# Attention and gated MLP on one core: K's first transposes moved ahead of x, weight loads held until x has landed, far loads held behind a copy of K

## The chip, the cores and the metric

One core of one Trainium2 chip. The metric is the device time of one execution in microseconds (us). Runs of one kernel mostly agree within 0.1%. In the lines of the profile PE is TensorE, PEld its weight loads, DVE VectorE, ACT ScalarE, POOL GpSimd and SP SyncE; L393 is line 393 of that run's kernel. A transfer lands when its data has arrived.

## The reference, cut to what matters

x is 2048 x 640. It is layer-normalised and goes into two branches: attention with 32 heads of size 192 against a cache of 2048 keys and values, and a gated MLP whose gate and up products share x.

```
xn = layernorm(x)
q = (xn @ wq) in 32 heads of 192;  p = softmax(q k^T / sqrt(192));  s = (p v) @ wo
g = silu((silu(xn @ w1) * (xn @ w3)) @ w2)
return x + s * g
```

## The kernel before

TensorE runs almost without a gap for 1.9 ms. Only the start concerns us: x, K and V of head 0 and the first weights must come in, x must be normalised and transposed, K transposed, before the first scores. TensorE does its part of it in program order.

```
def turn_over(k):                     # filler: keeps TensorE busy so that its clock rises
    for i in range(k):
        nc.tensor.matmul(warm, lhsT=ident_bf[:], rhs=ident_bf[:], start=True, stop=True)

def ln_turn(g, i2, copy):             # transposes two of the four tiles of an x group
    pst = ps_st.tile([P, 2, DC, P], BF16, tag="st2", name="pst")
    # ... 10 transposes into pst
    copy(out=xnT[:, :, q0:q0 + 2 * P]..., in_=pst[:])

def swap_halves(g):                   # xnS: the same x with its two partition halves exchanged
    qs = slice(g * 512, (g + 1) * 512)
    nc.sync.dma_start(out=xnS[0:64, :, qs], in_=xnT[64:P, :, qs])
    nc.sync.dma_start(out=xnS[64:P, :, qs], in_=xnT[0:64, :, qs])

def project_first():
    for hh in range(2):               # hh 0 reads the first half of x only
        hs = slice(hh * 256, (hh + 1) * 256)
        ps = ps_st.tile([P, 1024], F32, tag="st2", name="ps0")
        # ... 10 matmuls on xnT[:, c, hs], then casts by VectorE and ScalarE

def head_start():
    load_x(0, 0, 2); load_x(0, 2, 4); load_k0(0, nc.sync)
    load_w0()                         # three loads issued by GpSimd
    turn_over(44)
    # ... statistics of x
    load_k0(1, nc.scalar)             # K's second half
    load_x(1, queue=nc.scalar)        # the far loads: x of group 1 and half of V,
    load_v(0, (0,), nc.scalar)        # needed later
    # ... statistics, load_w(1), normalise
    ln_turn(0, 0, nc.scalar.copy)
    turn_k0(pk0, 0, range(4))         # 16 transposes: K's first half
    ln_turn(0, 1, nc.vector.tensor_copy)
    turn_k0(pk1, 1, (0, 1))           # 8 transposes: K's second half
    swap_halves(0)
    copy_k0(nc.scalar.copy, pk0, 0, 0)
    # ... two more copies of K, load_v(0, (1,)), load_x(2)
    project_first()
    # ... scores
```

The tiles pst, ps0 and the scores take turns in one pool of PSUM buffers (tag st2; PSUM is the memory that the matmuls here write to).

## Time and profile before

| | kernel before |
|---|---|
| time, median of its first 3 runs | 1938.25 us |
| span of the profiled run | 1936.4 us |
| TensorE busy | 1926.6 us |
| first projection, first scores, first product with V | 10.15, 13.10, 14.74 us |
| projection for head 1, projection of x group 1 | 18.84, 24.84 us |

The last row is times from the start of the span at which landmarks on TensorE begin. All waits of TensorE in the first 60 us (engine and line, what it waited for: us, times, longest):

```profile
PE pk L572 <- POOL ident_bf masks.py:199: 2.8, 1, 2.8
PE pst L354 <- DVE xn L346: 0.9, 1, 0.9
PE st L483 <- DVE qA L393: 0.2, 1, 0.2
```

There is not one wait for a transfer. That looks like slack, and it is not: the second view, a timeline of TensorE at head 1's projection (start, length, what), shows the first reader of xnS.

```profile
18.84 0.38 PE L424 MATMUL ps<-xnT,W 64*128 64x512 bf16 x1
19.05 0.39 PE L424 MATMUL ps<-xnS,W 64*128 64x512 bf16 x2
```

Matmuls on xnT and xnS are written as pairs on the two halves of the array. Here the xnS one starts 0.21 us after its partner: the second transfer of xnS, issued at 11.57, took 7.4 us to land, until about 19.0. Busy times by stretch (stretch, length, then the busy time of TensorE, its weight loads, VectorE, ScalarE and GpSimd with their instruction counts, granted clock, share of the DMA engines' time, GB/s):

```profile
5.00:6.00 1.00, 1.00 (x17) 1.00 (x16) 0.93 (x5) 0.97 (x3) 0.00 (x0) 1.00 0.99 298
6.00:7.00 1.00, 0.66 (x12) 0.49 (x9) 0.93 (x4) 0.45 (x2) 0.72 (x1) 1.00 0.74 155
```

### The profile page before, as it was taken

The page shows a single profiled execution, that of the slowest core. Times are in us where ns is not written, and L with a number is a line of the kernel's source. Part 1 is how long each engine was busy: PE and PEld are TensorE (multiplying, and loading weights), DVE is VectorE, ACT ScalarE, POOL GpSimd, SP SyncE. Part 2 cuts the span into 40 slices and gives each one's busy share as a digit, 9 for nine tenths or more (in the row PEclk, how much of TensorE's full clock was granted, in tenths as well). Part 3 has the DMA queues.
Part 4 walks back from the last instruction along what each step waited for, and adds up shares of the span by engine and source line. Part 5 has one row for each costly group of instructions (what it writes and reads, how often), then busy time and mean ns, then how long its engine had stood idle before and what let it go on. Part 6 is the DMA issues. An engine that isn't in the chain of part 4 may idle for free.

```text
span 1936.4 us, 59669 instructions
## 1 busy us (share of the span) xinstructions
PE 1926.6 (99%) x27273; PEld 1315.6 (68%) x27281; DVE 654.6 (34%) x997; ACT 1180.0 (61%) x1279; POOL 282.5 (15%) x501
## 2 busy tenths in 40 slices
PE   9999999999999999999999999999999999999998
PEld 6666666666666666666666666666666666577776
DVE  7333333333333333333333333333333334521111
ACT  6677676767676767776777777677767677210000
POOL 3111111111111111111111111111111110000000
PEclk9999999999999999999999999999999999999999
DMA  8643433323333434363434343434334220937783
GB/s 181 129 101 67 98 68 86 84 62 88 59 90 61 100 63 97 68 162 69 101 66 100 69 101 69 101 64 101 69 69 96 58 68 2 260 69 137 151 152 62
DMA packets 394643, 178.98 MB, mean 92 GB/s; under 512 B 341616, under 2 KB 382832, under 8 KB 394384
## 3 DMA queue, kind: packets, MB, share of 16 engines
q1 hardware_dynamic: 371136, 125.32, 31.6%
q0 software_dynamic: 19472, 45.71, 10.0%
q8 instruction: 215, 3.52, 0.8%
q10 hardware_dynamic: 3776, 4.06, 0.7%
q14 instruction: 44, 0.36, 0.1%
HBM read 52.82 MB, written 27.79 MB: 42 GB/s over the span
## 4 chain that ended last, share of the span: by engine, by line
PE 99%; DVE 1%; DMA 0%; ACT 0%; issue 0%; DVEq 0%; ACTq 0%
PE obank L519 35%; PE st L487 34%; PE ps L424 14%; PE ps_s L111 11%; PE ps_f L731 3%; PE ps_gu L705 1%; PE st L488 1%; PE ps L410 0%; DVE stats L316 0%; DMA x_all<-in_A_x_dram 0%; PE ps L391 0%; PE pst L354 0%; PE pk L271 0%; DVE xn L346 0%; ACT pT L493 0%
## 5 line engine op out<-in xcount | busy, mean ns | idle before, releaser
L493 ACT ACTIVATE pT<-st 128x1024 bf16<-128x1024 f32 (+1 forms) x1025 | 1046.1, 1021 | 250.2 <-PE st L488 234.0
L519 PEld LDWEIGHTS <-pT 64*128 64x128 bf16 x16384 | 711.3, 94 | 242.3 <-ACT pT L493 0.6
L519 PE MATMUL obank<-vt,pT 64*128 64x193 bf16 x16384 | 849.7, 243 | 0.0
L487 PE MATMUL st<-qC,KW 64*128 64x512 bf16 x2046 | 605.6, 376 | 0.1
L528 DVE COPY osum<-obank 128x772 f32<-128x772 f32 x128 | 123.1, 962 | 787.1 <-PE obank L519 787.1
L488 PE MATMUL st<-qB,KW 64*128 64x512 bf16 x1024 | 385.0, 376 | 0.0
L487 PE MATMUL st<-qA,KW 64*128 64x512 bf16 x1022 | 384.3, 376 | 0.1
L488 PE MATMUL st<-qC,KW 64*128 64x512 bf16 x1022 | 384.3, 376 | 0.0
L488 PE MATMUL st<-qA,KW 64*128 64x512 bf16 x1022 | 384.3, 376 | 0.0
L487 PEld LDWEIGHTS <-KW 64*128 64x128 bf16 x3068 | 278.5, 94 | 153.7 <-issue 2.1
L424 PE MATMUL ps<-xnT,W 64*128 64x512 bf16 x1280 | 297.2, 376 | 0.0
L424 PE MATMUL ps<-xnS,W 64*128 64x512 bf16 x1280 | 296.0, 376 | 0.0
L488 PEld LDWEIGHTS <-KW 64*128 64x128 bf16 x3068 | 278.5, 94 | 0.5
L377 POOL DMA_DIRECT2D qC<-qA x124 | 65.4, 528 | 1283.0 <-DVE rl_all L535 1268.2
L430 ACT CAST qB<-ps 128x512 bf16<-128x512 f32 x131 | 76.7, 585 | 228.2 <-PE ps L424 222.6
L111 PE MATMUL ps_s<-wo_sb,oT 128*128 128x384 bf16 (+3 forms) x1535 | 208.8, 299 | 0.1
L424 PEld LDWEIGHTS <-W 64*128 64x128 bf16 x2560 | 122.9, 94 | 121.4 <-issue 0.2
L111 PEld LDWEIGHTS <-oT 128*128 128x128 bf16 x1536 | 148.4, 98 | 60.4
L529 DVE TENSOR_TENSOR osum<-osum,obank 128x772 f32<-128x772 f32 x128 | 122.7, 959 | 13.4
L536 DVE TENSOR_TENSOR ostage<-osum,rl_all 128x768 bf16<-128x768 f32 x128 | 122.7, 958 | 6.3 <-DMA o_scr<-ostage 1.9
L465 DVE SCALAR_TENSOR_TENSOR hT<-pt,qB 64x512 bf16<-64x512 bf16 x64 | 43.8, 684 | 197.4 <-ACT pt L464 197.4
L429 DVE CAST qA<-ps 128x512 bf16<-128x512 f32 x131 | 90.6, 692 | 25.3 <-PE ps L410 7.2
(84 smaller groups left out, 621.9 us busy)
## 6 DMA issues: line engine op xcount, KB each, us to landing
o_scr<-ostage SPq DMA_DIRECT2D x16, 1536.0 KB, 10.6
vt<-in_A_v_cache_dram SPq DMA_DIRECT2D x63, 384.0 KB, 5.9
qC<-qA POOLq DMA_DIRECT2D x248, 64.0 KB, 1.9
qC<-qB POOLq DMA_DIRECT2D x124, 64.0 KB, 2.3
wo_sb<-in_A_wo_dram POOLq DMA_DIRECT2D x1, 7680.0 KB, 36.1
W<-in_A_wq_dram POOLq DMA_DIRECT2D x32, 160.0 KB, 3.6
W<-in_B_w_dram POOLq DMA_DIRECT2D x32, 80.0 KB, 3.3
W<-in_A_wq_dram POOLq DMA_DIRECT2D x32, 80.0 KB, 3.0
```

The source lines that it names most:

```text
L111: nc.tensor.matmul(ps[:, 0:w], lhsT=oT[:, k, :], rhs=wo_sb[:, k, c0:c1], start=(k == 0), stop=(k == OC - 1))
L377: nc.gpsimd.dma_start(out=qC[0:64, half, :], in_=qAB[half][64:P, :])
L424: nc.tensor.matmul(ps[:, r * 512:(r + 1) * 512], lhsT=W[rows, j, :], rhs=xs[rows, j // 2, qs], start=(j == 0), stop=(j == 2 * DC - 1))
L429: a = nc.vector.tensor_copy(out=qAB[0][:], in_=ps[:, 0:512])
L430: b = nc.scalar.copy(out=qAB[1][:], in_=ps[:, 512:1024])
L487: nc.tensor.matmul(st2[:, 0:512], lhsT=ka, rhs=qa, start=r == 0 and nr == 3, stop=r == nr - 1)
L488: nc.tensor.matmul(st2[:, 512:1024], lhsT=kb, rhs=qb2, start=r == 0 and nr == 3, stop=r == nr - 1)
L493: nc.scalar.activation(out=pT2[:, c * w:(c + 1) * w], in_=st2[:, c * w:(c + 1) * w], func=ACT.Exp, scale=att_scale)
L519: nc.tensor.matmul(obanks[r][:, j * 256:j * 256 + DH + 1], lhsT=pT2[r * 64:(r + 1) * 64, t * 512 + j * P:t * 512 + (j + 1) * P], rhs=vt[r ...
L528: nc.vector.tensor_copy(out=osum[:], in_=ov[0])
L529: nc.vector.tensor_tensor(out=osum[:], in0=osum[:], in1=ov[1], op=ALU.add)
L536: nc.vector.tensor_tensor(out=ostage[:, qb * 4:qb * 4 + 4, hg * DH:(hg + 1) * DH], in0=osum[:, :, 0:DH], in1=rl.unsqueeze(2).to_broadcast( ...
```

## The change

The intent: K's first half needs nothing from x, so it is turned while TensorE would only run filler. To make it land early, weights are held back until x has landed (a two-column copy on GpSimd that reads x stands before them), and the far loads stand behind ScalarE's first copy of K. The filler reads a constant tile that is ready earlier, and becomes longer.

```diff
+    fill = const.tile([P, P], BF16, name="fill")
+    nc.vector.memset(fill[:], 1.0)
...
+    gate = const.tile([P, 2], BF16, name="gate")
...
-            nc.tensor.matmul(warm, lhsT=ident_bf[:], rhs=ident_bf[:], start=True, stop=True)
+            nc.tensor.matmul(warm, lhsT=fill[:], rhs=fill[:], start=True, stop=True)
...
         load_k0(0, nc.sync)
+        nc.gpsimd.tensor_copy(out=gate[:], in_=x_sb[:, 0, 0:2])
         load_w0()
-        turn_over(44)
+        turn_over(60)
+        pk0 = ps_o.tile([P, 4, 512], BF16, tag="ob0", name="pk0")
+        turn_k0(pk0, 0, range(4))
...
         load_k0(1, nc.scalar)
+        copy_k0(nc.scalar.copy, pk0, 0, 0)
         load_x(1, queue=nc.scalar)
         load_v(0, (0,), nc.scalar)
...
-        pk0 = ps_o.tile([P, 4, 512], BF16, tag="ob0", name="pk0")
         ln_turn(0, 0, nc.scalar.copy)
-        turn_k0(pk0, 0, range(4))
+        turn_k0(pk1, 1, (0, 1))
         ln_turn(0, 1, nc.vector.tensor_copy)
-        turn_k0(pk1, 1, (0, 1))
         swap_halves(0)
-        copy_k0(nc.scalar.copy, pk0, 0, 0)
```

## The prediction

> **What bounds the kernel now.** I read the page first, then the chain of waits that ended last, cut to the start, then the timeline of the first 15 us with the transfers of the same stretch. The page's busy shares and its chain, shares by engine:
>
> ```profile
> PE 1926.6 (99%) x27273; PEld 1315.6 (68%) x27281; DVE 654.6 (34%) x997; ACT 1180.0 (61%) x1279; POOL 282.5 (15%) x501
> ...
> PE 99%; DVE 1%; DMA 0%; ACT 0%; issue 0%; DVEq 0%; ACTq 0%
> ```
>
> TensorE is busy 1926.6 of 1936.4 us, so all its idle time together is 9.8 us, half a per cent. The change touches no instruction of the steady loop; it can only win in the start, so I read the chain there (start us, length us, what):
>
> ```profile
> 0.75 2.81 DMA x_all<-in_A_x_dram
> 3.58 0.90 DVE stats L316 x2
> ...
> 7.13 0.06 DVE ve L590
> 7.19 0.36 DVE xn L346
> 7.55 0.05 issue
> 7.60 0.81 PE pst L354 x10
> 8.41 0.89 PE pk L271 x16
> 9.30 0.56 PE pst L354 x10
> 9.86 0.45 PE pk L271 x8
> 10.31 2.20 PE ps L391 x20
> 12.51 0.02 issue
> 12.53 0.42 DVE qA L393
> ```
>
> The start has three links. The first load of x lands at 0.75 + 2.81 = 3.56. VectorE then works without a hole on layer-norm statistics (3.58 to 7.19) and on the normalised tiles xn. From 7.60 TensorE works in program order: the first half of x turned, 16 transposes of K's first half (pk, 0.89), the second half of x, 8 of K's second half, and the first projection (L391), after whose casts the first scores start at 13.10. So the 16 transposes of K, which need nothing from x, stand in the path after x. Where the second half of x ended its wait shows in the timeline (start, busy, what):
>
> ```profile
> 8.13 0.90 DVE L346 TENSOR_SCALAR xn<-x_all,mv,rstd 128x640 bf16<-128x640 bf16 x2 [0.23 <-POOL rstd L327]
> 8.45 1.23 ACT L356 COPY xnT<-pst 128x1280 bf16<-128x1280 bf16 x1 [2.00 <-PE pst L354]
> ```
>
> xn is complete at 9.03, and ScalarE's copy of the first half of x, which the first projection reads, at 9.68. Both are limits that remain if K's transposes leave. Last, the transfers between 0 and 4.8 us, then 4.8 and 7.0 us (queue: packets, MB, share):
>
> ```profile
> q1 hardware_dynamic: 368, 0.90, 57.5%
> W<-in_A_wq_dram POOLq DMA_DIRECT2D x1, 160.0 KB, 6.1
> W<-in_A_wq_dram POOLq DMA_DIRECT2D x1, 80.0 KB, 4.6
> ...
> q0 software_dynamic: 146, 0.31, 52.8%
> q1 hardware_dynamic: 64, 0.15, 22.1%
> ```
>
> Until 4.8 us SyncE's queue (q1: x and K's first half) moves alone. The weights, though issued by GpSimd from 1.30 on, appear only after that, on q0, and then take over half of the engines' time while the last 0.15 MB of K's first half trickle in: that load, issued at 1.68, needs 6.0 us and lands at 7.7.
>
> **What the Trainium skill says.** "DMA: Bandwidth & Descriptors", section "Issuing engines are not separate DMA queues": transfers issued from SyncE, ScalarE and GpSimd run on the same 16 DMA engines and interleave. The trace agrees for K's first half (above). It does not show the weights hurting x: they moved nothing until x had landed. Same page, section "Anatomy of one DMA": "any semaphore wait happens on the issuing sequencer before dispatch". So the new one-column copy on GpSimd, which waits for x, holds back the three weight loads behind it, and ScalarE's copy of K, waiting for TensorE, holds back the loads of x and V behind it; this trace has no such pair. "TensorE: Matmul & The Clock Gate", Part 1: the array runs at half clock until it has been busy for about 3.4 us. The trace agrees: the filler starts at 2.77, its matmuls take 314 ns at first and 219 at the end, with last start at 6.4, and all later transposes take 219.
>
> **The change part by part.**
>
> (1) *Filler on a constant tile, 60 instead of 44.* It waited for the identity matrix, which GpSimd finishes at 2.72 behind a weight issue (1.30 to 2.32). A VectorE fill of 128x128 right after 0.82 should take some 0.15 us (the 128x16 one takes 0.07), so TensorE starts near 1.1. Cold pairs come every 83 ns (12 per us in the windows of the trace), so 60 last 5.0 us if cold throughout: end 5.5 to 6.1, instead of 6.66. The array is warm when real work begins, as before. Worth nothing by itself: no wait on this filler is on the path.
>
> (2) *Weights behind x.* Their issues move from 1.30 to 3.65 (x at 3.56 plus a tiny copy), 1.02 + 0.89 + 0.87 = 2.78 us, until 6.43. x lands no earlier, since nothing of theirs ran beside it. K's first half, whose packets had the engines to themselves until about 5, should land near 5.8 instead of 7.7. Two debts. GpSimd's first rstd waits until 6.43 instead of running at 6.00; 6.43 + 0.72 = 7.15 is still before VectorE is free at 7.19, and the second rstd needs 7.19 anyway: cost 0 to 0.1. And the weights land later: in the trace 6.1, 5.2 and 4.6 us after issue under load, 3.6, 3.3 and 3.0 as medians of the run; from issues at 3.65, 4.67 and 5.56 that is 8.6 to 10.2 for the last.
>
> (3) *K's first half before x.* With K at 5.8 and the filler over at 6.0, the 16 transposes take 0.93 and end near 7.0, inside TensorE's present hole (6.66 to 7.60). They leave the path: -0.89. But the program now puts the 8 transposes of K's second half before the second half of x. That second half of K is issued by ScalarE at 5.53 as before and landed at 9.1 (3.6 us) beside part of the x load; now it shares the engines with the 0.33 MB of weights but no longer with x and V. Its 0.39 MB plus the weights at the some 340 GB/s of that stretch is 2.1 us from its first packets at about 6.6: my estimate is a landing at 8.6 to 9.0. So: first half of x 7.60 to 8.41, wait for K to about 8.8, 8 transposes 0.45 to 0.55 to 9.3, x's second half (xn complete at 9.03) 0.56 to 9.9, first projection at 9.9 to 10.0. Before: 10.31. Net -0.35. The floor is ScalarE's xnT copy at 9.68, so no more than -0.6 whatever K does.
>
> (4) *Far loads behind ScalarE's first K copy.* The copy runs near 7.0 to 8.0, before the x copy at 8.45, which it does not delay if the issues (0.45 + 0.70) run beside it, as they ran beside an activation before. The loads of x (group 1) and V leave near 7.1 instead of 5.96, about 1.2 us later. V would land near 13.3 to 13.9; its first reader is at 14.7. The x group is read at 14.29 and landed at 10.8. Both have slack: cost 0. ScalarE's second K copy ends earlier, so the first cast no longer queues behind it (11.44 before), which is not on the path.
>
> Sum: -0.35 in the first projection, and the rest of the start (casts 12.53, scores 13.10, exponentials 14.08) shifts with it, since from there on the chain is made of engine work only. A few hundredths come from hiding K's last 8 transposes no better than before. I put the whole at -0.4 of 1938.25.
>
> **The rivals.**
>
> *The weights become the last wait.* First projection waits for weights at 10.2, or for the second part a little later: gain 0 to 0.1, time 1938.2. For it: the landings of 4.6 to 6.1 us in this very stretch. Against: those loads shared the engines with x and K's first half, and the run's medians are 3.0 to 3.6.
>
> *K's second half is the last wait.* If it lands at 9.6 because the weights now move beside it, the whole second half of x waits behind it in order: projection at 10.7, time 1938.6. For it: the new order on TensorE. Against: twice its bytes were on its queue before, and it still landed at 9.1.
>
> *x lands earlier* because GpSimd no longer works beside it. Then everything moves: 0.3 more, 1937.5. Against: no weight packet before 4.8.
>
> *The gain is swallowed later*, at the waits around 28 to 34 us where ScalarE and VectorE are in the chain. Against: these are chains of engine work, which begin earlier too.
>
> **Range and chances.** Expected gain 0.45 with rival three's chance weighed in: 1937.8. Uncertainty of the mechanism about 0.4, of a median of three some 0.4 (the runs spread from 1937.86 to 1939.1): range 1936.9 to 1938.7. Two per cent is 39 us, and the whole start, before the first scores, lasts 13. No rival comes near it; only a changed clock over the whole run could. Chances: faster 0.005, within 2% 0.99, slower 0.005.
>
> **What would show it.** In the changed kernel: filler starts near 1.1 (step 1); weight issues begin near 3.6 and rstd near 6.4 (2); K's first transposes end near 7.0, before the first transposes of x at about 7.6; the first projection begins at 9.7 to 10.1 (3); first scores near 12.7. It is wrong if the weight loads on TensorE's projection, or K's second half ahead of x's, take a wait of over 0.5 us, or if x lands at a time other than 3.5 to 3.6.

## The result, and the profile after

The changed kernel takes 1941.0 us (median of 6, 1939.79 to 1943.84) against 1938.24 for the kernel before (6 runs, 1937.86 to 1939.1). The ratio is 1.0015, interval 1.0002 to 1.0028: within 2%, but about 2.8 us slower where 0.45 faster was predicted.

The waits of TensorE in the first 60 us of the changed kernel:

```profile
PE pk L575 <- DVE fill L297: 1.1, 1, 1.1
PE ps L393 <- DVE xnT L358: 1.0, 1, 1.0
PE obank L521 <- DMA vt<-in_A_v_cache_dram: 0.8, 1, 0.8
PE pk L271 <- DMA kn<-in_A_k_cache_dram: 0.8, 1, 0.8
PE ps L412 <- DMA xnT<-xn: 0.2, 1, 0.2
```

Three of the five lines are transfers, where there were none. The start in order of time (timeline of all engines, cut):

```profile
1.06 6.27 PE L575 MATMUL pk<-fill 128*128 128x128 bf16 x60 [1.06 <-DVE fill L297]
...
7.17 1.06 PE L271 MATMUL pk<-ident_bf,kn 128*128 128x128 bf16 x16
...
9.65 0.62 PE L271 MATMUL pk<-ident_bf,kn 128*128 128x128 bf16 x8 [0.78 <-DMA kn<-in_A_k_cache_dram]
...
10.87 0.82 DVE L358 COPY xnT<-pst 128x1280 bf16<-128x1280 bf16 x1 [1.48 <-PE pst L356]
...
11.84 2.35 PE L393 MATMUL ps<-xnT,W 128*128 128x256 bf16 x20 [1.01 <-DVE xnT L358]
...
17.32 0.84 PE L521 MATMUL obank<-vt,pT 64*128 64x193 bf16 x16 [0.83 <-DMA vt<-in_A_v_cache_dram]
```

The filler runs to 7.3 us, K's first half is turned from 7.17 on, its second half lands at 9.61 and takes 0.78 us of wait, VectorE copies the second half of x from 10.87 to 11.69, and only then does the first projection start, at 11.84 instead of 10.15. At 17.32 the first product with V has waited 0.83 for V. The same two stretches as before show what happened to the transfers:

```profile
5.00:6.00 1.00, 1.00 (x12) 1.00 (x11) 0.93 (x4) 0.97 (x3) 1.00 (x3) 1.00 0.34 70
6.00:7.00 1.00, 1.00 (x13) 1.00 (x11) 0.97 (x4) 0.40 (x2) 0.98 (x2) 1.00 0.56 175
```

From 5 to 7 us the DMA engines are used 34% and 56% of the time, where they had been used 99% and 74%. Work that stood in that stretch is done later, on top of what comes there anyway. Bytes moved by 8, 12 and 20 us, summed from the trace's transfers: 1.73, 2.99 and 4.74 MB before, 1.47, 2.62 and 4.08 after. The first half of V (issuing queue, KB, us from issue to landing), before and then after:

```profile
vt<-in_A_v_cache_dram ACTq DMA_DIRECT2D x1, 384.0 KB, 6.3
```

```profile
vt<-in_A_v_cache_dram ACTq DMA_DIRECT2D x1, 384.0 KB, 8.6
```

It is issued at 8.64 instead of 6.44 and lands at about 17.3 instead of 12.7. The second transfer of xnS lands at 12.53 + 9.0 = 21.5 instead of 19.0; its reader begins at 21.62, 0.36 after its partner on the array.

From the projection of x group 1 on (27.53 us, 2.69 later than before) the two kernels run in parallel: the spans differ by 2.6. This holds for all variants below. Span minus the start of that projection is 1911.4 to 1911.6 us in 19 of 20 profiles (in e14 0.9 more, not followed up), so that landmark accounts for the whole difference between the profiled runs.

### The profile page after: what moved, and what is told of

Read it like the earlier page. It is cut to its first block, busy times and chain, and to the rows that moved or that the text cites. A ratio compares the mean times of both kernels' runs of the same rounds, so it can differ in the third digit from the quotient of the medians. Undisturbed runs are those within 1.5% of the kernel's fastest.

```text
span 1939.0 us, 59712 instructions
## 1 busy us (share of the span) xinstructions
PE 1929.8 (100%) x27297; PEld 1319.6 (68%) x27297; DVE 654.8 (34%) x998; ACT 1180.1 (61%) x1279; POOL 282.1 (15%) x502
## 3 DMA queue, kind: packets, MB, share of 16 engines
q0 software_dynamic: 19472, 45.71, 10.2%
## 4 chain that ended last, share of the span: by engine, by line
PE 98%; DMA 1%; DVE 1%; ACT 0%; issue 0%; SPq 0%; DVEq 0%; ACTq 0%
PE obank L521 35%; PE st L489 33%; PE ps L426 14%; PE ps_s L111 11%; PE ps_f L735 3%; PE ps_gu L709 1%; PE st L490 0%; PE ps L412 0%; DMA xnT<-xn 0%; DMA kn<-in_A_k_cache_dram 0%; DVE stats L318 0%; DMA x_all<-in_A_x_dram 0%; PE ps L393 0%; DVE xn L348 0%; DVE mv L319 0%
## 5 line engine op out<-in xcount | busy, mean ns | idle before, releaser
L111 PE MATMUL ps_s<-wo_sb,oT 128*128 128x256 bf16 (+3 forms) x1536 | 208.8, 300 | 0.0
```

Of the source, the lines that this page charges most:

```text
L111: nc.tensor.matmul(ps[:, 0:w], lhsT=oT[:, k, :], rhs=wo_sb[:, k, c0:c1], start=(k == 0), stop=(k == OC - 1))
```

## The experiments

All variants gave correct results. Landmarks are from each variant's profile, in us; the ratio is to the kernel before of the same rounds. The kernel before had medians of 1938.17 to 1938.39.

| run | median us | ratio | first projection | first V product | x group 1 | span |
|---|---|---|---|---|---|---|
| before | 1938.24 | | 10.15 | 14.74 | 24.84 | 1936.4 |
| after | 1941.00 | 1.0015 | 11.84 | 17.32 | 27.53 | 1939.0 |
| e1 | 1939.76 | 1.0010 | 12.56 | 19.28 | 29.04 | 1940.5 |
| e2 | 1939.99 | 1.0021 | 10.83 | 15.34 | 26.68 | 1938.2 |
| e3 | 1940.54 | 1.0016 | 11.30 | 17.41 | 27.01 | 1938.5 |
| e4 | 1940.29 | 1.0013 | 10.78 | 15.67 | 26.92 | 1938.4 |
| e5 | 1939.81 | 1.0008 | 12.15 | 16.73 | 26.50 | 1938.0 |
| e6 | 1939.49 | 1.0004 | 10.30 | 14.89 | 26.45 | 1937.9 |
| e7 | 1940.01 | 1.0013 | 10.93 | 16.00 | 26.64 | 1938.2 |
| e8 | 1939.76 | 1.0008 | 10.33 | 16.05 | 26.55 | 1938.0 |
| e9 | 1938.93 | 1.0002 | 11.67 | 16.18 | 25.94 | 1937.4 |
| e10 | 1938.28 | 1.0000 | 10.40 | 14.99 | 25.41 | 1936.9 |
| e11 | 1939.87 | 1.0011 | 10.61 | 16.14 | 26.79 | 1938.3 |
| e12 | 1938.97 | 1.0003 | 10.56 | 15.07 | 25.74 | 1937.2 |
| e13 | 1939.37 | 1.0005 | 10.19 | 14.78 | 26.08 | 1937.6 |
| e14 | 1939.75 | 1.0006 | 10.39 | 14.98 | 26.27 | 1938.7 |
| e15 | 1940.58 | 1.0011 | 11.50 | 17.48 | 27.24 | 1938.7 |
| e16 | 1939.43 | 1.0005 | 9.94 | 14.67 | 26.19 | 1937.7 |
| e17 | 1937.91 | 0.9998 | 10.39 | 14.98 | 24.74 | 1936.1 |
| e18 | 1938.02 | 0.9999 | 9.99 | 14.65 | 24.41 | 1935.8 |

The intervals of the ratios are about 0.0013 to either side, so single pairs of neighbours are not told apart by them; most runs of a variant lie within 0.5 us of its median, and the medians together with the landmarks carry the argument. The plainest comparisons are of whole sets: in their own rounds all five runs of e5, e7, e8 and e11, and four of e6's five, lie above all nine of the kernel before, and all five of e9 lie below all six of the changed kernel.

### Undoing one part of the change at a time

**e1, far loads early again.**

```diff
-        copy_k0(nc.scalar.copy, pk0, 0, 0)
         load_x(1, queue=nc.scalar)
         load_v(0, (0,), nc.scalar)
+        copy_k0(nc.scalar.copy, pk0, 0, 0)
```

> The changed kernel with one part undone: ScalarE issues the loads of x (group 1) and V ahead of its first K copy again. Theory of four separate losses (the one I hold: K's second half ahead of x about 0.6 us, a swapped PSUM buffer about 1.0, V late 0.8, a DMA transpose 0.2): the wait of the first value matmul for V (0.83 us) goes, V lands before 14 us, the first projection still starts at 11.6 to 12.0, total about 0.8 to 1.1 us below the changed kernel, so near 1940 and still over 1939. Rival (the far loads are the whole loss, since they also hold back ScalarE's copy of x): first projection back near 10.3 and the time back at 1938.2.

Two of its five runs took 1942.3, three 1939.5 to 1939.8. The profile is of one of the slow two, and shows something that is in neither kernel's profile (busy by stretch, as above; the eighth column is the granted clock):

```profile
7.00:8.00 1.00, 0.00 (x0) 0.00 (x0) 0.80 (x5) 0.86 (x1) 1.00 (x2) 1.00 0.89 126
...
9.00:10.00 1.00, 0.05 (x1) 0.05 (x2) 0.46 (x2) 1.00 (x1) 1.00 (x2) 1.00 1.04 421
...
12.00:14.00 2.00, 1.44 (x7) 1.02 (x8) 1.01 (x2) 0.00 (x0) 0.00 (x0) 0.50 1.25 208
```

```profile
12.56 4.43 PE L393 MATMUL ps<-xnT,W 128*128 128x256 bf16 x20 [1.01 <-DVE xnT L358]
```

TensorE stood idle from 7 to 8 us and nearly so from 9 to 10, and from 10.54 to 17.37 (clock records of the trace) it was granted half its clock: 20 matmuls took 4.43 us instead of 2.35. No wait for V is left; this alone would prove little, since the lost clock moved the first product with V to 19.28, but V also lands at about 14.3 instead of 17.3. So the far loads' delay makes V late. The median without it is 1.2 us lower, which the intervals of the two ratios don't tell apart; the "lost clock" is a separate hazard of the changed start.

**e2, K's second half behind x again.**

```diff
-        turn_k0(pk1, 1, (0, 1))
         ln_turn(0, 1, nc.vector.tensor_copy)
+        turn_k0(pk1, 1, (0, 1))
```

> The changed kernel with K's second half turned behind the second half of x again, as before. Theory of four losses: the second half of x is turned at about 9.4 to 10.0 instead of 10.28 to 10.85, first projection 0.7 to 0.9 us earlier (10.9 to 11.1, still held by VectorE's copy of the second half of x), the V wait grows by as much, because V lands at 17.2 whatever TensorE does, so the total gains 0 to 0.3 us only. Rival (order on TensorE is the whole loss): 1.6 us off, 1939.2 or less.

The first projection starts at 10.83, 1.0 earlier, with 0.6 us of wait left for VectorE's copy of x, and the wait for V is gone. In its place TensorE waits 0.9 us for xnS. Three runs lie at 1939.6 to 1940.0, two at 1944.7 and 1945.8. The order of K and x is worth about 1 us at the first projection, and gives way to a transfer. That the wait for V is gone is not shown to come from this edit: in this profile full clock came at 4.91 and the filler ended at 6.40 (6.86 and 7.33 in the changed kernel's), so V was issued at 7.71 instead of 8.64. The same goes for e4 (4.89; V issued at 7.70) and e15 (4.41; 7.48).

**e3, weights early again.**

```diff
-        nc.gpsimd.tensor_copy(out=gate[:], in_=x_sb[:, 0, 0:2])
         load_w0()
```

> The changed kernel without the copy that holds the first weights back. Theory of four losses: K's first half lands near 7.7 as before instead of 5.9, its 16 transposes run 7.7 to 8.6 in front of x and everything after is 0.3 to 0.8 later, while K's second half lands 0.3 to 0.6 earlier (near 9.1); total within 0.6 us of the changed kernel, either side. Rival (holding the weights back is the loss, because they then move beside K's second half): K's second half lands by 8.6, first projection at 10.8 or earlier, 1 us or more off the time.

K's first half now takes 5.0 us to land (6.7 us) and is waited for, 0.7 us; K's second half lands at 9.07 instead of 9.61, and the first projection starts at 11.30, 0.5 earlier than in the changed kernel. V still comes late, with 1.5 us of wait. Holding the weights back is not what makes V late.

**e4, the copies of the two halves of x exchanged between engines.**

```diff
-        ln_turn(0, 0, nc.scalar.copy)
+        ln_turn(0, 0, nc.vector.tensor_copy)
         turn_k0(pk1, 1, (0, 1))
-        ln_turn(0, 1, nc.vector.tensor_copy)
+        ln_turn(0, 1, nc.scalar.copy)
```

> The changed kernel with VectorE copying the first half of x out of PSUM and ScalarE the second, which gives the first product of the projection the buffer of the first half again (the built program shows it; no other way to get it back was found). Theory of four losses: the first projection starts right behind the second transposes of x, at 10.8 to 11.0 instead of 11.84 (about 0.9 earlier), its second product waits for ScalarE's slower copy (1.23 us), so that the first scores come 0.4 to 0.8 earlier than 14.71; the V wait takes that back: total 0 to 0.3 us off. Rival (the buffer does not matter, the projection really needs the whole of x): the start stays at 11.8 or later and the first scores come later than 14.7.

This tests a term that I had overlooked. The built program shows which PSUM buffer a tile takes (bank 0 for the first product in before and e4, bank 2 in after and e2, with the first half of x in bank 0 and the second in bank 2 in all four). In the kernel before the first product takes the buffer of the first half of x, which ScalarE had copied out by 9.68; with K's transposes moved it takes the buffer of the second half, and so waits for VectorE's copy of the second half, though it reads only the first. With the engines exchanged the two products are (start, length, what, wait):

```profile
10.78 1.26 PE L393 MATMUL ps<-xnT,W 128*128 128x256 bf16 x10
12.25 1.25 PE L393 MATMUL ps<-xnT,W 128*128 128x256 bf16 x10 [0.22 <-ACT xnT L358]
```

The projection starts 1.06 earlier, before ScalarE's copy of the second half of x has even begun (10.98). The 0.2 us of wait is the second product's, which does read that half. But the scores come only at 14.02, and xnS takes 0.9 us of wait: 0.6 us of gain in the span, 0.7 in the median.

**e7 and e8, two and three of these at once.** e7 is e1's and e2's edits, e8 adds e4's.

> The changed kernel with two parts undone: far loads ahead of ScalarE's first K copy, and K's second half behind the second half of x. My theory: first projection at 10.7 to 11.0 (VectorE's copy of the second half of x still holds it, the buffer is still swapped), no wait for V and none of 0.9 us for the swapped halves of x, so 0.6 to 0.8 us over the kernel before: 1938.8 to 1939.1 in executions without a half-speed stretch. Rival (the transfers are late because of the weights, not of the far loads): the 0.9 us wait for the swapped halves of x stays and the time is 1939.5 or more.

> As the run before, and VectorE copies the first half of x and ScalarE the second, which gives the first product the buffer of the first half again. What is left of the change is the constant filler, the held-back weights and K's first half in front of x. My theory: first projection at 9.7 to 10.0, first scores at 12.7 to 13.2, time 1937.8 to 1938.5, equal to the kernel before. Rival (K in front of x cannot pay, whatever the buffer): first projection after 10.3, time 1938.8 or more.

Both missed what I expected. e7 took 1940.01, with 0.6 us of wait for VectorE's copy, 0.5 for xnS (as the rival had it) and 0.4 for the last weights. In e8 the first projection begins at 10.33, nearly as before. It then waits 1.0 us for the last weights, which land at about 12.0, and 0.3 for xnS:

```profile
12.09 1.80 PE L393 MATMUL ps<-xnT,W 128*128 128x256 bf16 x15 [1.05 <-DMA W<-in_A_wq_dram]
```

Of the moved loads only the weights are still held back, and the time is 1.5 us above before. What the prediction called the first rival (weights become the last wait) is real here, but not in the changed kernel, where the last weights land at 9.9. In the profiles with the weights held back they land at 11.9 to 12.2 where the far loads are early (e1, e5, e7, e8, e11) and at 9.5 to 9.9 where these are held back too (after, e2, e4, e15): with the far loads back in front, the gate of the weights costs more.

**e9, both moves of loads undone, order and filler as in the changed kernel** (e1's and e3's edits).

> The changed kernel with both moves of loads undone (first weights at once, far loads ahead of ScalarE's K copy); TensorE's new order, the filler and the swapped buffer stay. Theory of transfers (new, from the runs so far: until about 20 us the transfers are the second bound, and what is not moved between 5 and 10 us is missing when the second projection needs the swapped halves of x): 1.7 MB are moved by 8 us and 2.9 or more by 12 us as before, no wait for V, first projection at 11.2 to 11.6 because of order and buffer, total 0.8 to 1.6 us over the kernel before, and no more than 0.6 us of wait for the swapped halves. Rival (order and buffer alone explain the loss, the loads cost nothing): same time as the changed kernel, 1940 or more.

```profile
PE pk L271 <- DMA kn<-in_A_k_cache_dram: 1.4, 1, 1.4
...
PE ps L393 <- DVE xnT L358: 1.0, 1, 1.0
```

The median is 1938.93, 0.7 above before. The first projection is as late as in the changed kernel (11.67), yet 2.1 of the 2.8 us are gone: so the two moves of loads together cost most of the loss. The 0.7 us that is left lies within the noise of the kernel before, and order, exchanged buffers and filler are all still there: how it is shared between them is not shown.

### One part alone, on the kernel before

**e5 and e11, the gate of the weights alone**, with 44 and with 60 fillers on the identity.

```diff
+        gate = const.tile([P, 2], BF16, name="gate")
+        nc.gpsimd.tensor_copy(out=gate[:], in_=x_sb[:, 0, 0:2])
         load_w0()
-        turn_over(44)
+        turn_over(60)          # e11 only
```

> The kernel before with one part of the change alone: the first weights are held back until x has landed, nothing else. My theory: the last first-weight load lands at 9.5 to 10.2, first projection starts within 0.2 us of 10.15, K's second half lands 0.3 to 0.6 later (near 9.5, its transposes run at 9.65, so no wait), time within 0.5 us of the kernel before (1938.2). Rival (the late weights cause the loss, by crowding the far loads and the transfers behind them): first projection after 10.5 or a wait for V or for the swapped halves of x, time over 1939.2.

> The kernel before with the first weights held back and 60 fillers instead of 44, so that the clock is not lost as it was with 44. Theory of transfers and late weights: the last first-weight load lands at 11.5 to 12.2, because the far loads, early here, crowd it; the second product of the first projection waits for it by 0.8 to 1.5 us; time 1939.2 to 1940. Rival (with 44 fillers the lost clock was the whole loss): no wait for weights, 1938.0 to 1938.6.

Both are 1.6 us slower, where I had expected 0.5 at most of e5. In e5 the identity is ready earlier (no weight issue stands ahead of it), so the filler ends at 5.68, TensorE stands until 8.00, and the clock is at half from 8.35 to 11.76. In e11 the longer filler closes that hole, the clock holds, and the loss comes from the weights: 0.8 us of wait in the projection, 0.5 for xnS. Two ways to lose the same time.

**e6 and e10, 60 fillers on a constant tile, and the constant tile made but not used.**

```diff
+    fill = const.tile([P, P], BF16, name="fill")
+    nc.vector.memset(fill[:], 1.0)
-            nc.tensor.matmul(warm, lhsT=ident_bf[:], rhs=ident_bf[:], start=True, stop=True)   # e6 only
+            nc.tensor.matmul(warm, lhsT=fill[:], rhs=fill[:], start=True, stop=True)           # e6 only
-        turn_over(44)                                                                          # e6 only
+        turn_over(60)                                                                          # e6 only
```

> The kernel before with 60 fillers on the constant tile, nothing else. The filler starts at 1.07 and ends between 5.3 and 7.2 us, wherever the clock turns full (the executions so far turned at 3.7 to 6.9 us). My theory: x is turned at 7.6 as before, time within 0.4 us of 1938.2, and no execution with a half-speed stretch, since the work behind it is as dense as before. Rival (the early filler spoils the clock: it ends earlier and leaves a longer hole before x): executions of 1941 and more, as the changed kernel has them.

> The kernel before with the constant tile made and filled but not used: only the addresses behind it move by 256 bytes and VectorE does one fill of 0.17 us more. Tests why the constant filler alone came out at 1939.5 in four of five executions. If the layout or the fill is the cause: 1939.2 or more in most executions, with the second half of the swapped x landing after 20 us. If not (what I expect): 1937.8 to 1938.5 in most, and the swapped half lands at 19.

The tile itself costs nothing in the median (1938.28), though in its profile xnS landed at 19.6, not at 19 as expected. The fillers alone, off every path, cost 1.2 us in four of five runs (1939.24 to 1939.70; the fifth took 1937.8). First projection and first V product are within 0.15 of before; the whole loss is one wait on TensorE, at head 1's projection, and no stretch at half clock, which my rival had expected:

```profile
19.00 0.38 PE L426 MATMUL ps<-xnT,W 64*128 64x512 bf16 x1
20.80 0.39 PE L426 MATMUL ps<-xnS,W 64*128 64x512 bf16 x2 [1.43 <-DMA xnS<-xnT]
```

**e12, K's first half in front, everything else as close to before as can be**: e3's, e1's, e2's and e4's edits together.

> Of the change only the constant filler and K's first half in front of x are left, with loads as before, K's second half behind x, and the two copies of x swapped between VectorE and ScalarE so that the first product keeps its buffer. K's first half lands at 6.7 to 7.7 here. Theory of transfers: first scores at 12.6 to 13.3, but the swapped halves of x still land at 18.6 to 20.7, so the time is 1938.0 to 1939.5, no better than the kernel before. Rival (K in front is worth its 0.9 us of TensorE work once nothing else is in the way): 1937.5 or less.

K's first half, issued at 1.68, is still slow to land beside the weights (0.9 us of wait), then x is turned at once. First scores come at 13.42, just later than I expected; 1938.97, no gain.

### Is the late landing of xnS a cause?

From before to e12 the projection of x group 1 began 5.65 to 5.94 us after the first reader of xnS, and in ten of these fourteen profiles that reader had its transfer to wait for (landing at 19.0 before, 20.7 in e6, 21.5 after; in e1, e3, e5 and e9 xnS had landed before its turn). That could be a companion. The next runs replace the transfers of swap_halves for group 0 by copies inside the chip.

**e13, e14, e15, e16: both transfers replaced by GpSimd copies**, in e6, the kernel before, the changed kernel, and e12.

```diff
     def swap_halves(g):
+        if g == 0:
+            nc.gpsimd.tensor_copy(out=xnS[0:64, :, qs], in_=xnT[64:P, :, qs])
+            nc.gpsimd.tensor_copy(out=xnS[64:P, :, qs], in_=xnT[0:64, :, qs])
+            hold = const.tile([P, 4], BF16, name="hold")      # keeps the loads behind it in place
+            nc.sync.dma_start(out=hold[:], in_=xnT[:, 0, 254:258])
+            return
```

> The kernel before with 60 fillers on a constant tile (as e6), but the swapped copy of the first x group is made by two GpSimd copies inside the chip instead of two transfers. e6 took 1939.49, with a wait of 1.4 us for the transferred swapped half. Theory (the landing of that half sets the start): the wait goes and the time returns to 1938.0 to 1938.5, first scores at 13.2 or so as in e6. Rival (the landing only goes along with something else): the wait moves to another releaser and the time stays at 1939.2 to 1939.7.

> The kernel before with the swapped copy made by GpSimd. There the landing came at 18.97 and its first reader ran at 19.05, so nothing waits. Theory: no gain, 1937.9 to 1938.4. If the landing had bound before as well, 1937.4 or less. Rival (GpSimd's copies, slow, become the wait): 1938.8 or more, with a wait of the scores on GpSimd.

> The changed kernel with the swapped copy made by GpSimd. Theory (two things are late, TensorE's own order by 1.6 us and the far loads by another 1 us): the V wait of 0.8 us stays or grows, so the time falls by 0 to 0.5 us only, to 1940.3 to 1940.8 in executions without the lost clock. Rival (the swapped half alone makes the loss): 1939.3 or less.

> K's first half in front, loads as before, K's second half behind x, casts swapped (as e12, 1938.97), with the swapped copy made by GpSimd. In e12 first scores were at 13.42 with 0.3 us of wait on the transferred half. Theory: the 0.3 us goes, 1938.4 to 1938.8; as first scores are no earlier than before, it can't beat 1938.25. Rival (the front order wins once the transfers are out of the way): 1937.6 or less.

e13 stayed at 1939.37, as the rival had it, and the kernel before lost 1.4 us (e14). The wait for xnS did go in e13: both matmuls of head 1's first pair start at 19.56, where in e6 the second started at 20.80. But a wait of 0.8 us on VectorE came later. The timeline of e13 shows why:

```profile
13.31 2.31 POOL L368 COPY xnS<-xnT 64x2560 bf16<-64x2560 bf16 x1
...
13.45 2.32 DVE L408 COPY qC<-qA 64x512 bf16<-64x512 bf16 x1
...
15.80 0.29 DVE L409 COPY qC<-qA 64x512 bf16<-64x512 bf16 x1
```

VectorE's copy of 64 x 512, 0.29 us in the kernel before, took 2.32 and ended within 0.15 us of GpSimd's copy. The Trainium skill, "SBUF — State Buffer", section "SBUF: two separate sides", says that VectorE in some of its modes and GpSimd share a pair of ports under an exclusive lock, where the second fully blocks; the trace agrees. Everything of VectorE's behind it, statistics of the next x group above all, came 2 us later. So e13 to e16 changed two things, and decide nothing about the cause. In e15 the wait for V is gone too (see e2), and TensorE waits 1.4 us for VectorE instead; in e16 the first scores start at 12.80, 0.3 ahead of the kernel before, and that is lost again in the same way.

**e17 and e18: only the second transfer replaced**, in e6 and e12. GpSimd's one copy ends at 13.46 in e17; of VectorE's copies only the first, at 13.23, still meets it and takes 0.38 us.

```diff
     def swap_halves(g):
+        if g == 0:
+            nc.sync.dma_start(out=xnS[0:64, :, qs], in_=xnT[64:P, :, qs])
+            nc.gpsimd.tensor_copy(out=xnS[64:P, :, qs], in_=xnT[0:64, :, qs])
+            return
```

> As e13 (before, 60 constant fillers), but only the second half of the swap is made by GpSimd, the first stays a transfer. In e13 GpSimd's second copy (13.31 to 15.62) held up a copy on VectorE (2.32 us where the kernel before has 0.29), which came back as a wait of 0.8 us. GpSimd's one copy should be over at 13.3, ahead of VectorE's copies. Theory (the late second swapped half is the cause of e6's loss): no wait on the swapped half, no wait on VectorE, 1937.9 to 1938.7. Rival (the fillers themselves cost the time elsewhere): 1939.2 or more, as e6 and e13.

> As e16 (K's first half in front, loads as before, K's second half behind x, casts swapped), again with only the second half of the swap made by GpSimd. e16's first scores came at 12.80 (before 13.10) and were given back to VectorE's locked copy. Theory: the gain of up to 0.3 us stays, 1937.7 to 1938.4, at best a tie with before. Rival: 1938.9 or more, because K's first half, which ends its wait at 7.3 to 8.0, still pushes x back.

e17 fell from e6's 1939.49 to 1937.91, e18 from e12's 1938.97 to 1938.02, each with all five runs below the median of its sibling (on another chip, but the kernel before was as fast there: 1938.17, against 1938.26). The pair of matmuls starts together now (e17):

```profile
19.09 0.38 PE L430 MATMUL ps<-xnT,W 64*128 64x512 bf16 x1
19.09 0.59 PE L430 MATMUL ps<-xnS,W 64*128 64x512 bf16 x2
```

The late landing of xnS was the cause of what the fillers cost: it was the only wait that e6 had on top. (e17 also takes 320 KB out of the transfers; why they land late in e6 stays open.) As a side result, the pair runs without its skew: from head 1's projection to that of x group 1 it takes 5.65 us in e17 and e18, 6.00 in the kernel before and 7.45 in e6. Neither version is told apart from the kernel before (ratios 0.9998 and 0.9999, intervals of 0.0014 to either side), so no variant is shown to beat it.

## Why the prediction was wrong, point by point

The steps that failed most are 2 and 4, which gave both moves of loads a cost of 0 to 0.1 us: without them 2.1 of the 2.8 us are gone (e9). Step 3 had the sign of the first projection wrong, through K's later landing and a buffer that it did not know of.

**What bounds the kernel.** Right that only the start matters, and that the rest runs in parallel. Wrong that the start is a chain of engine work with transfers only at its head: "chains of engine work, which begin earlier too" was read from a wait list with no transfer in it. xnS had no slack (landing at about 19.0, partner at 18.84). That list is blind to one half of the array that waits while the other works.

**Step 1, the filler: mis-sized.** "Cold pairs come every 83 ns" was read from counts of 12 per window, which include instructions cut by the window's edges; starts in that trace are 107 ns apart at first. Measured: 60 pairs in 6.3 us in the changed kernel, nearly all at half clock, some 105 ns each. It ended at 7.3 instead of 5.5 to 6.1. The 60 took 4.88 us in e6, where the clock came at 4.0, and 6.20 in e17, where it came at 6.7: the length depends on when full clock is granted, and no single number was right. The prediction's "the trace agrees" holds for the step from half to full clock, not for the 3.4 us: by the clock record of the kernel before, full clock came at 5.45, 2.7 us after the filler began. "Worth nothing by itself" failed too: in e6 it cost 1.2 us.

**Step 2, weights behind x: K's landing right, the debts wrong.** K's first half landed at 5.9 (predicted 5.8) and the issues ran from 3.98 to 6.77 (3.65 to 6.43). x itself landed at 3.81, outside the 3.5 to 3.6 that the prediction named (3.6 to 3.9 across the profiles), and xn was complete at 9.40 instead of the 9.03 that the prediction took over. The weights were not a wait of the changed kernel (landing 9.9, predicted 8.6 to 10.2), but are when the far loads go back in front (e7, e8, e11), and the gate alone costs 1.6 us.

**Step 3, the order on TensorE: the sum failed, -0.35 predicted, +1.69 measured.** Its terms: K's second half landed at 9.61, not 8.6 to 9.0. That is the second rival, which had been given 9.6 and a projection at 10.7. The 1.1 us beyond that is the exchanged PSUM buffer, of which neither step nor rival spoke: the named floor was "ScalarE's xnT copy at 9.68"; the real one was VectorE's copy, ending at 11.69. e4 shows it (10.78), and e2 that K's place is worth 1.0. ScalarE's own copy, put behind K's copy, ended at 10.53, so the named floor was off as well.

**Step 4, far loads: "Both have slack: cost 0" failed.** That a wait on the issuing engine holds back the loads behind it, as the prediction cites, is what the changed kernel shows: ScalarE issues them at 8.27 and 8.64, beside its copy of K, which began at 8.26. But V landed at about 17.3, not at 13.3 to 13.9. The issue came at 8.64 rather than near 7.1, because it stands behind K's transposes, which stood behind the filler (with an earlier full clock it came at 7.7, in e2 and e4); and the landing took 8.6 us rather than 6.3 as before. Undoing this move alone (e1) lowers the median by 1.2 us, which is not clear of noise.

**The missing term.** In its first 20 us the start is limited by transfers as well as by TensorE. Both gates take work out of a stretch where it was free (5 to 7 us: DMA share 0.99 and 0.74, then 0.34 and 0.56) and put it where the engines were full. e9 shows the size: 2.1 of 2.8 us. e17 shows the way for the last link, the landing of xnS.

**The range** assumed 0.4 us of uncertainty about the mechanism; the exchanged buffer (1.0 us), late V (0.8), late xnS (0.3 to 1.4) and the lost clock were not in it.

**Open.** Why the fillers alone make xnS land 1.7 us later in most runs (by the medians it is not the added tile, e10). Whether the runs 3 to 6 us above the others in after, e2, e3, e4, e7 and e11 are the lost clock of e1: it fits, but none of them was profiled. The record gives 1945.84 of e2, and 1941.23 of the changed kernel, a mean granted clock of 0.998, as e1's slow two; 0.999 occurs in undisturbed runs too and tells nothing. So the lost clock may be in some of the runs behind the 1941.0. It is not in the profiled one, which took 1940.77. The far loads were never moved alone on the kernel before.

## What to carry to other kernels

Here gates that held transfers back were paid with DMA time that was missing later: before adding one, look whether the DMA engines have other work for the stretch it empties. No wait for a transfer in the list is not slack: subtract landing from first use for each transfer near the path. And when tiles share a pool, moving one instruction changes which buffer the next tile gets, and with it which engine it waits for; read the wait list of the built program before predicting.

## What the Trainium skill lacked or had wrong

- "TensorE: Matmul & The Clock Gate", Part 1: half clock returns after an idle window of some 3.4 us, by its table. In e1 the window before the loss (7.13 to 10.54) held about 1.4 us of busy TensorE, two fifths of it, and the longest hole beside it was 1.2 us; in e5 one third of the window was busy. So a window that is partly busy loses the clock too, and the page gives no share of busy time at which that happens. On the way up, with windows of 3.41 us counted back from the change of the clock, 2.65 us of busy TensorE (e1) were enough for full clock, and 2.39 (the changed kernel's first window) were not. Its lengths agree: 3.41 us of half clock in e5, 6.83 (twice that) in e1; and so does the free-running start, which gave full clock 2.6 us after the filler began in e1 and 5.8 in the changed kernel.
- "DMA: Bandwidth & Descriptors", "Anatomy of one DMA — SWDGE (gpsimd) path": its fit of 2.0 us plus bytes at 436 GB/s gives, as an estimate, 2.9 us for 384 KB and 2.8 for 320 KB. The page's fit is for another issue path. In the two kernels here the first load of x (320 KB) took 2.8 us in the kernel before, and the transfers of these sizes behind it, with other loads in flight, took up to 9.8 us. No page that we know says how to size a landing under load.
- No page: the profile's wait list does not show a wait of one half of the array while the other works (0.21 us before and 0.36 after are not in it; between e17 and the kernel before that stretch differs by 0.35 us).
- No page: which buffer of a pool a tile takes decides on whom it waits (the first product of the projection waited 1.0 us in e9 and not at all in e4).
